# Sigmoid attention and SwiGLU feed-forward: the weights' fp32-to-fp16 conversion moved from VectorE and GpSimd instructions into the weight DMAs

## The chip, the cores and the metric

The kernel runs on one core of one Trainium2 chip. The metric is the device time of one execution in microseconds (us), where lower is better. A profile of one execution, taken by the hardware profiler, accompanies the times. In it PE is TensorE's matmul side, PEld its weight load, DVE is VectorE, ACT is ScalarE, POOL is GpSimd and SP is SyncE, which here issues DMAs only. The names SPq and POOLq stand for DMA-issuing instructions on the queues of those engines.

## The reference

Inputs are `q`, `k`, `v` of shape 8 x 12 x 448 x 64 (batch, heads, sequence, head width) and three weight matrices, all fp32:

```
scores = q @ k.T / sqrt(64) - log(448)
attn   = sigmoid(scores)            # no softmax: every score alone
x      = (attn @ v), heads side by side -> 3584 x 768
g      = x @ w_gate                 # 768 x 1536
val    = x @ w_val                  # 768 x 1536
out    = (g * sigmoid(g) * val) @ w_out      # 1536 x 768 -> 3584 x 768, fp32
```

## The kernel before

**Tiling.** Four heads of one batch make a group, so there are 24 groups `n`, three to a batch. A group has seven tiles `c`. For each tile TensorE computes scores (`qk_tile`, L146), ScalarE takes the sigmoid from PSUM to an fp16 tile `pt` (L157), and after the seventh tile `pv` (L169) multiplies by `v` and VectorE copies the result to the fp16 tiles `xT` (L179). When a batch's three groups are done, the feed-forward runs on it in units: twelve blocks `f` of 128 hidden columns, each with a gate unit and a value unit of six matmuls (L195). The gate unit is followed by a sigmoid on ScalarE (L200) and a product on VectorE (L202), the value unit by a second product on VectorE (L207) that writes `hT`. Output units (L222) follow after each pair of batches. VectorE scales their results to fp32 (L229) and GpSimd's queue stores them (L237).

**Loading q, k and v.** SP issues three DMAs per group (L97), 448 KB each, into six fp32 buffers `st`. VectorE, ScalarE or GpSimd casts each to 16 bit (L115, L117): q and k to bf16 tiles `c`, v to an fp16 tile. q and k are then transposed to tiles `T`: for groups 0 to 5 by TensorE through PSUM (L129) and a VectorE copy (L133), and from group 6 on by a transposing DMA that SP issues (L122).

**Loading weights.** Each of the three matrices comes in six pieces of 768 KB. SP issues the DMA (L81) into one of three fp32 staging buffers `wst`. Later a cast instruction (L87) on VectorE or GpSimd writes the fp16 tiles `wg`, `wv` and `wo` that the matmuls read. These fp16 tiles stay for the whole kernel.

**What sets the order.** The program is written out in one order and every engine works through its own instructions in that order, each waiting for its inputs and for its output buffer to be free. A prologue does the attention of batch 0 (groups 0 to 2). Then a loop over feed-forward units starts, into which two-tile attention steps of later batches are put by a table of nominal unit durations (1.13 and 1.95). Inside the feed-forward of batch 0 the 21 tiles of groups 3 to 5 are spread. The first step with a tile of group 6 comes after the gate unit of block `f` = 9.

SP's order is the list `order`, in which loads of q, k, v and of weights alternate. It is advanced by `loads(...)` calls at fixed points of the prologue and, in the unit loop, after each weight cast and each second tile of a group. A weight load that waits for one of the three staging buffers holds back all that stands behind it in SP's order, and a weight cast that waits for its DMA holds back all that stands behind it on VectorE or GpSimd. In the unit loop, the casts of group `n`+1 are placed at the second tile of group `n`.

Of the kernel before, what the change touches and what calls it, by code (L numbers as in the profile page):

```python
# [17 lines left out]
def kernel(  # L18
# [45 lines left out]
    make_identity(nc, idn)  # L64


    wg16 = [one.tile([128, NP, 256], FP16, tag=f"wg{i}", name=f"wg16_{i}") for i in range(NF // 2)]
    wv16 = [one.tile([128, NP, 256], FP16, tag=f"wv{i}", name=f"wv16_{i}") for i in range(NF // 2)]
    wo16 = [one.tile([128, 2, DM], FP16, tag=f"wo{i}", name=f"wo16_{i}") for i in range(NF // 2)]
    wstage = {}  # L70

    def w_load(kind, i):
        st = wst.tile([128, 1536], FP32, tag="wst", name=f"wst_{kind}{i}")
        if kind == "o":
            src = moe_w_out[i * 256:(i + 1) * 256, :].rearrange("(f p) n -> p f n", p=128)
            dst = st.rearrange("p (f n) -> p f n", f=2)
        else:
            w = moe_w_gate if kind == "g" else moe_w_val
            src = w[:, i * 256:(i + 1) * 256].rearrange("(j p) n -> p j n", p=128)
            dst = st.rearrange("p (j n) -> p j n", j=NP)  # L80
        nc.sync.dma_start(out=dst, in_=src)  # L81
        wstage[(kind, i)] = st

    def w_cast(kind, i, eng):
        dst = {"g": wg16, "v": wv16, "o": wo16}[kind][i]
        st = wstage.pop((kind, i))
        eng.tensor_copy(out=dst.rearrange("p a b -> p (a b)"), in_=st)  # L87


    qkv_st = {}  # L90
# [98 lines left out]

    def ffn1(b, f, gate):  # L190
        ps = psG.tile([128, S], FP32, tag="G", name="ps_g" if gate else "ps_vl")
        w = (wg16 if gate else wv16)[f // 2]
        cs = slice((f % 2) * 128, (f % 2) * 128 + 128)
        for pr in range(NP):
            nc.tensor.matmul(  # L195
                out=ps, lhsT=w[:, pr, cs], rhs=xT[(b, pr)], start=(pr == 0), stop=(pr == NP - 1)
            )
        if gate:
            s16 = tmp.tile([128, S], FP16, tag="s16", name="s16")
            nc.scalar.activation(out=s16, in_=ps, func=SIGM)  # L200
            t1 = tmp.tile([128, S], FP16, tag="t1", name="t1")
            nc.vector.tensor_tensor(out=t1, in0=ps, in1=s16, op=MULT)  # L202
            gcur[0] = t1
        else:
            if b % 2 == 0:
                hT[(b // 2, f)] = htp.tile([128, 2, S], FP16, tag="hT", name=f"hT_{b // 2}_{f}")
            nc.vector.scalar_tensor_tensor(  # L207
                out=hT[(b // 2, f)][:, b % 2, :], in0=ps, scalar=HSC, in1=gcur[0], op0=MULT, op1=MULT
            )
# [3 lines left out]
    def ffn2(b, m, half):  # L213
# [5 lines left out]
        for f in range(NF):  # L219
            h = hT[(b // 2, f)].rearrange("p b s -> p (b s)")  # L220
            lhsT = h[:, m * 128:(m + 1) * 128]
            nc.tensor.matmul(  # L222
                out=o,
                lhsT=lhsT,
                rhs=wo16[f // 2][:, f % 2, half * hw:(half + 1) * hw],
                start=(f == 0),
                stop=(f == NF - 1),
            )
# [49 lines left out]
    NPE = 2 * NJ  # L278


    order = []
    for n in range(NJ):
        order += [(n, 0), (n, 1), (n, 2)]
    order += [("g", 0), ("v", 0), (3, 0), (3, 1), ("g", 1), ("v", 1), (3, 2)]
    order += [("g", 2), ("v", 2), (4, 0), (4, 1), (4, 2), ("g", 3), ("v", 3)]
    order += [(5, 0), (5, 1), (5, 2), ("g", 4), ("v", 4), ("g", 5), ("v", 5)]
    order += [("o", 0), ("o", 1), (6, 0), (6, 1), (6, 2), ("o", 2), ("o", 3), ("o", 4), ("o", 5)]
    order.reverse()

    def loads(n):  # L290
        for _ in range(n):
            if order:
                a, b_ = order.pop()
                if isinstance(a, str):
                    w_load(a, b_)
                else:
                    load(a, b_)


    loads(6)  # L300
# [6 lines left out]
    cast(1, 0, nc.gpsimd)  # L307
    cast(1, 1, nc.vector)
    cast(1, 2, nc.gpsimd)
    loads(3)  # L310
    b0 = [(n, c) for n in range(NJ) for c in range(C)]
    for n, c in b0:
        attn_step([(n, c)], [n - 1] if c == 2 and n > 0 else [])
        if (n, c) == (0, 1):
            trans_pe(1, 0)
            trans_pe(1, 1)
            loads(1)
        if (n, c) == (0, 3):
# [4 lines left out]
        if (n, c) == (1, 1):  # L323
            trans_pe(2, 0)
            trans_pe(2, 1)
        if (n, c) == (1, 3):
            w_cast("g", 0, nc.vector)
            w_cast("v", 0, nc.vector)
            loads(3)
        if (n, c) == (2, 0):  # L330
            cast(3, 0, nc.gpsimd)
            cast(3, 1, nc.gpsimd)
            loads(2)
        if (n, c) == (2, 2):
            w_cast("g", 1, nc.vector)
            w_cast("v", 1, nc.gpsimd)
            cast(3, 2, nc.gpsimd)
            loads(3)
        if (n, c) == (2, 3):
            trans_pe(3, 0)  # L340
            trans_pe(3, 1)
    pv(NJ - 1)


    wcq = [("g", 2), ("v", 2), ("g", 3), ("v", 3), ("g", 4), ("v", 4), ("g", 5), ("v", 5)]
    wcq += [("o", i) for i in range(6)]
    wk = 0
    loaded, casted = 7, 4
    tcur = 0.0
    vi = 0  # L350
    pend = []
    for ui, (dur, u) in enumerate(units):
        while vi < len(visits) and tcur >= vtime[vi]:
            group = visits[vi]
            vi += 1
# [2 lines left out]
            for n, c in group:  # L358
                if c == C - 1:
                    pend.append(n)  # L360
                if c == 1:
                    nn = n + 1
                    loads(3)
# [23 lines left out]
        else:  # L387
            ffn2(*u[1:])
        tcur += dur
        while wcq and ui + 1 >= 1.75 * wk:  # L390
            kind, i = wcq.pop(0)
            w_cast(kind, i, nc.gpsimd if kind == "v" or kind == "o" and i % 2 else nc.vector)
            loads(2)
            wk += 1


# [28 lines left out]
```

## Time and profile before

| | us |
|---|---|
| time, median of 3 (lowest to highest) | 470.07 (469.03 to 471.04) |
| time of the profiled execution | 469.27 |
| its span on the core | 467.5 |
| PE busy | 427.2 (91%) |
| DVE busy | 227.9 (49%) |
| ACT busy | 211.0 (45%) |
| POOL busy | 103.9 (22%) |

The span runs from the first to the last recorded instruction; 1.8 us of the execution's time lies around it. Busy shares are averages over stages that have different limits. The profile also cuts the span into 40 slices of 11.7 us, with the busy tenths of each engine, the clock that TensorE was granted (in tenths of full speed), the busy share of the core's 16 DMA engines and the rate of their transfers. Windows of any length can be asked for in the same form. A chain of waits, followed back from the last instruction, says at each step what released it. A list in order of time gives every instruction's start and duration with, in square brackets, how long its engine sat idle before it and who ended that.

### The profile page before, as it was taken

The page shows a single profiled execution, that of the slowest core. Times are in us where ns is not written, and L with a number is a line of the kernel's source. Part 1 is how long each engine was busy: PE and PEld are TensorE (multiplying, and loading weights), DVE is VectorE, ACT ScalarE, POOL GpSimd, SP SyncE. Part 2 cuts the span into 40 slices and gives each one's busy share as a digit, 9 for nine tenths or more (in the row PEclk, how much of TensorE's full clock was granted, in tenths as well). Part 3 has the DMA queues.
Part 4 walks back from the last instruction along what each step waited for, and adds up shares of the span by engine and source line. Part 5 has one row for each costly group of instructions (what it writes and reads, how often), then busy time and mean ns, then how long its engine had stood idle before and what let it go on. Part 6 is the DMA issues. An engine that isn't in the chain of part 4 may idle for free.

```text
span 467.5 us, 7908 instructions
## 1 busy us (share of the span) xinstructions
PE 427.2 (91%) x3252; PEld 213.9 (46%) x3252; DVE 227.9 (49%) x369; ACT 211.0 (45%) x267; POOL 103.9 (22%) x139
## 2 busy tenths in 40 slices
PE   3779594499999999999999999999999999999993
PEld 2344241244455544444455544444455545555661
DVE  2367373066454355655642454665544356555321
ACT  4776264145643446465534355656543451222000
POOL 2323423620014364100032353200004100000121
PEclk9989888599999999999999999999999999999998
DMA  8986988994006589900027869810014410000232
GB/s 284 349 268 241 355 285 278 306 280 146 1 21 160 165 221 313 281 27 1 1 53 212 237 167 299 237 20 1 1 35 109 101 35 1 1 1 0 68 100 70
DMA packets 66757, 66.97 MB, mean 143 GB/s; under 512 B 35745, under 2 KB 63393, under 8 KB 66721
## 3 DMA queue, kind: packets, MB, share of 16 engines
q1 hardware_dynamic: 64032, 55.45, 40.7%
q0 software_dynamic: 2688, 11.01, 8.7%
q8 instruction: 25, 0.41, 0.3%
q14 instruction: 12, 0.09, 0.1%
HBM read 47.19 MB, written 11.01 MB: 124 GB/s over the span
## 4 chain that ended last, share of the span: by engine, by line
PE 84%; DMA 7%; DVE 3%; ACT 2%; issue 1%; SPq 1%; POOL 1%; POOLq 0%; ACTq 0%; DVEq 0%
PE ps_o L222 24%; PE ps_vl L195 23%; PE ps_g L195 22%; PE ps_sc L146 8%; PE ps_pv L169 6%; ACT pt L157 2%; DMA wst_g<-in_moe_w_gate_dram 2%; DMA wst_o<-in_moe_w_out_dram 2%; DMA st<-in_q_dram 1%; DMA T<-c 1%; PE ps_tr L129 1%; DVE xT L179 1%; SPq L97 1%; DVE hT L207 0%; SPq L122 0%
## 5 line engine op out<-in xcount | busy, mean ns | idle before, releaser
L157 ACT ACTIVATE pt<-ps_sc,sb_t 128x896 f16<-128x896 f32 x168 | 159.7, 1006 | 108.6 <-PE ps_sc L146 108.6
L195 PE MATMUL ps_vl<-xT,wv 128*128 128x448 f16 x576 | 127.1, 357 | 5.1 <-DVE hT L207 5.1
L195 PE MATMUL ps_g<-xT,wg 128*128 128x448 f16 x576 | 126.7, 356 | 1.5 <-DVE xT L179 1.4
L222 PE MATMUL ps_o<-wo,hT 128*128 128x384 f16 x672 | 113.5, 326 | 0.0
L202 DVE TENSOR_TENSOR t<-ps_g,s 128x448 f16<-128x448 f32 x96 | 59.9, 624 | 82.8 <-ACT s L200 81.8
L200 ACT ACTIVATE s<-ps_g 128x448 f16<-128x448 f32 x96 | 52.2, 544 | 106.1 <-PE ps_g L195 106.1
L237 POOL DMA_DIRECT2D out_dram<-osb x56 | 29.2, 525 | 257.3 <-DVE osb L229 257.3
L222 PEld LDWEIGHTS <-hT 128*128 128x128 f16 x672 | 64.0, 98 | 48.6 <-issue 7.9
L195 PEld LDWEIGHTS <-wv 128*128 128x128 f16 x576 | 54.7, 99 | 65.0 <-issue 18.0
L195 PEld LDWEIGHTS <-wg 128*128 128x128 f16 x576 | 54.6, 99 | 58.5 <-issue 12.0
L207 DVE SCALAR_TENSOR_TENSOR hT<-ps_vl,t 128x448 f16<-128x448 f32 x96 | 60.0, 625 | 30.4 <-PE ps_vl L195 22.7
L179 DVE CAST xT<-ps_pv 64x448 f16<-64x448 f32 x96 | 59.7, 622 | 24.4 <-PE ps_pv L169 23.0
L146 PE MATMUL ps_sc<-T,T 64*64 64x448 bf16 x672 | 52.5, 379 | 19.4 <-DMA T<-c 12.7
L229 DVE TENSOR_SCALAR osb<-ps_o 128x384 f32<-128x384 f32 x56 | 31.2, 558 | 74.6 <-PE ps_o L222 74.4
L117 POOL CAST c<-st 128x896 bf16<-128x896 f32 x44 | 40.7, 938 | 38.7 <-DMA st<-in_q_dram 29.7
L169 PE MATMUL ps_pv<-pt,v 64*64 64x448 f16 x672 | 37.3, 357 | 0.3 <-ACT pt L157 0.3
L146 PEld LDWEIGHTS <-T 64*64 64x64 bf16 x672 | 13.8, 107 | 51.1 <-issue 36.6
L117 POOL CAST v<-st 128x896 f16<-128x896 f32 x24 | 22.5, 936 | 35.9 <-PE ps_pv L169 22.4
L169 PEld LDWEIGHTS <-v 64*64 64x64 f16 x672 | 20.4, 109 | 12.9 <-issue 1.3
L129 PE MATMUL ps_tr<-idn,c 128*128 128x128 bf16 x84 | 8.7, 276 | 6.4 <-DVE c L117 4.6
L87 POOL CAST wv<-wst_v 128x1536 f16<-128x1536 f32 x5 | 7.3, 1469 | 18.2 <-DMA wst_v<-in_moe_w_val_dram 18.2
L129 PEld LDWEIGHTS <-c 128*128 128x128 bf16 x84 | 6.9, 125 | 9.4 <-DVE c L117 4.8
(16 smaller groups left out, 27.7 us busy)
## 6 DMA issues: line engine op xcount, KB each, us to landing
st<-in_q_dram SPq DMA_DIRECT2D x24, 448.0 KB, 4.4
st<-in_k_dram SPq DMA_DIRECT2D x24, 448.0 KB, 5.6
st<-in_v_dram SPq DMA_DIRECT2D x24, 448.0 KB, 6.3
out_dram<-osb POOLq DMA_DIRECT2D x56, 192.0 KB, 3.1
wst_g<-in_moe_w_gate_dram SPq DMA_DIRECT2D x6, 768.0 KB, 9.5
wst_v<-in_moe_w_val_dram SPq DMA_DIRECT2D x6, 768.0 KB, 5.1
wst_o<-in_moe_w_out_dram SPq DMA_DIRECT2D x6, 768.0 KB, 4.8
T<-c SPq DMA_TRANSPOSE x36, 5.4
```

Source lines behind the costliest of these rows:

```text
L117: eng.tensor_copy(out=o, in_=i)
L146: nc.tensor.matmul(out=sc[w * 64:(w + 1) * 64, h2, :S], lhsT=kt[r, c, w * 64:(w + 1) * 64], rhs=qt[r, :, w * 64:(w + 1) * 64], start=True, ...
L157: nc.scalar.activation(out=pt, in_=sc[:, :, :S], func=SIGM, bias=sb_t, scale=qkscale)
L169: nc.tensor.matmul(out=P[w][h2 * 64:(h2 + 1) * 64, :], lhsT=vt[r, h2, c * D:(c + 1) * D], rhs=pt[r, h2, :], start=(c == 0), stop=(c == C - 1),
L179: nc.vector.tensor_copy(out=x[w * 64:(w + 1) * 64, :], in_=P[w][h2 * 64:(h2 + 1) * 64, :])
L195: nc.tensor.matmul(out=ps, lhsT=w[:, pr, cs], rhs=xT[(b, pr)], start=(pr == 0), stop=(pr == NP - 1))
L200: nc.scalar.activation(out=s16, in_=ps, func=SIGM)
L202: nc.vector.tensor_tensor(out=t1, in0=ps, in1=s16, op=MULT)
L207: nc.vector.scalar_tensor_tensor(out=hT[(b // 2, f)][:, b % 2, :], in0=ps, scalar=HSC, in1=gcur[0], op0=MULT, op1=MULT)
L222: nc.tensor.matmul(out=o, lhsT=lhsT, rhs=wo16[f // 2][:, f % 2, half * hw:(half + 1) * hw], start=(f == 0), stop=(f == NF - 1),)
L229: nc.vector.tensor_scalar(out=osb[:, half * hw:(half + 1) * hw], in0=o, scalar1=HREC, scalar2=None, op0=MULT)
L237: nc.gpsimd.dma_start(out=dst, in_=osb[i * 64:(i + 1) * 64, :])
```

## The change

The staging buffers `wst`, the DMAs into them and all cast instructions of the weights are removed. GpSimd's queue issues DMAs whose source is the fp32 matrix and whose destination is the fp16 tile. Each matrix now comes in four pieces of 1152 KB (three blocks `f` each) instead of six of 768 KB (two blocks). There are twelve such DMAs. The eight for `w_gate` and `w_val` name 128 x 6 rows of 384 numbers, the four for `w_out` name 128 x 3 rows of 768 numbers.

With this, the schedule of loads is written anew. The number of `st` buffers goes from six to nine. SP's list holds q, k and v loads (and transposes) alone, with three groups loaded ahead. The casts of group `n`+2, no longer of `n`+1, stand at the second tile of group `n`, and with them the transposing DMAs from group 6 on. In the prologue, the first weight DMAs stand on GpSimd behind the casts of q of group 1 and v of group 0, and each later pair behind the casts of the next group. TensorE's transposes of groups 1 and 2 stand two tiles later than before. One cast of k (group 3) goes from GpSimd to VectorE.

```diff
-    stg = ctx.enter_context(tc.tile_pool(name="stg", bufs=6))
-    wst = ctx.enter_context(tc.tile_pool(name="wst", bufs=3))
+    stg = ctx.enter_context(tc.tile_pool(name="stg", bufs=9))
...
+    FW = 3
+    NW = NF // FW
...
     def w_load(kind, i):
-        st = wst.tile([128, 1536], FP32, tag="wst", name=f"wst_{kind}{i}")
...
-        nc.sync.dma_start(out=dst, in_=src)
-        wstage[(kind, i)] = st
-
-    def w_cast(kind, i, eng):
...
-        eng.tensor_copy(out=dst.rearrange("p a b -> p (a b)"), in_=st)
+        cs = slice(i * FW * 128, (i + 1) * FW * 128)
         if kind == "o":
+            nc.gpsimd.dma_start(out=wo16[i], in_=moe_w_out[cs, :].rearrange("(f p) n -> p f n", p=128))
+        else:
+            w, dst = (moe_w_gate, wg16[i]) if kind == "g" else (moe_w_val, wv16[i])
+            nc.gpsimd.dma_start(out=dst, in_=w[:, cs].rearrange("(j p) n -> p j n", p=128))
...
+    load3(0)
+    load3(1)
+    load3(2)
     cast(0, 0, nc.vector)
     cast(0, 1, nc.scalar)
+    cast(1, 0, nc.gpsimd)
     cast(0, 2, nc.gpsimd)
     trans_pe(0, 0)
     trans_pe(0, 1)
...
     cast(1, 1, nc.vector)
+    w_load("g", 0)
+    w_load("v", 0)
+    load3(3)
     cast(1, 2, nc.gpsimd)
...
                 if c == 1:
-                    nn = n + 1
-                    loads(3)
-                    if loaded <= nn + 1 < NQ and not order:
-                        for w in (0, 1, 2):
-                            load(nn + 1, w)
+                    nn = n + 2
+                    if loaded <= nn + 1 < NQ:
+                        load3(nn + 1)
                         loaded = nn + 2
...
+                    for _ in range(2):
+                        if wl:
+                            w_load(*wl.pop(0))
...
-        while wcq and ui + 1 >= 1.75 * wk:
-            kind, i = wcq.pop(0)
-            w_cast(kind, i, nc.gpsimd if kind == "v" or kind == "o" and i % 2 else nc.vector)
-            loads(2)
-            wk += 1
```

Two pieces of the order show what moves. In them `st_6_680` is a staging buffer for group 6 (the last number only names the buffer), `c_0_6` the bf16 tile of q (0) or k (1) of group 6, `v_6` its v, and `T_6` a transposed tile.

On SP, from the loads of group 5 to the transposes of group 6, the rows before are:

```order
L97 DMA st_5_548<-in_v_dram 128x2x448
L81 DMA wst_g_568<-in_moe_w_gate_dram 128x6x256
L81 DMA wst_v_570<-in_moe_w_val_dram 128x6x256
L81 DMA wst_g_582<-in_moe_w_gate_dram 128x6x256
L81 DMA wst_v_584<-in_moe_w_val_dram 128x6x256
L81 DMA wst_o_621<-in_moe_w_out_dram 128x2x768
L81 DMA wst_o_623<-in_moe_w_out_dram 128x2x768
L97 DMA st_6_680<-in_q_dram 128x2x448
L97 DMA st_6_682<-in_k_dram 128x2x448
L97 DMA st_6_710<-in_v_dram 128x2x448
...
L97 DMA st_7_951<-in_v_dram 128x2x448
L122 DMA_TRANSPOSE T_6_957<-c_0_6_953 128x7x128
```

and now:

```order
L88 DMA st_5_454<-in_v_dram 128x2x448
L88 DMA st_6_535<-in_q_dram 128x2x448
L88 DMA st_6_537<-in_k_dram 128x2x448
L88 DMA st_6_539<-in_v_dram 128x2x448
L88 DMA st_7_741<-in_q_dram 128x2x448
L88 DMA st_7_743<-in_k_dram 128x2x448
L88 DMA st_7_745<-in_v_dram 128x2x448
L113 DMA_TRANSPOSE T_6_751<-c_0_6_747 128x7x128
```

All weight loads, ten of them between the loads of group 5 and the transposes of group 6, have left SP's order; the loads of group 7 still stand ahead of the transposes of group 6.

On GpSimd, from its first cast to the casts of group 6, now:

```order
L108 CAST c_0_1_134<-st_1_118 128x2x7x64
L108 CAST v_0_136<-st_0_116 128x896
L78 DMA wg_0_100<-in_moe_w_gate_dram 128x6x384
L78 DMA wv_0_104<-in_moe_w_val_dram 128x6x384
L108 CAST v_1_168<-st_1_122 128x896
L108 CAST c_0_2_218<-st_2_124 128x2x7x64
...
L78 DMA wv_3_107<-in_moe_w_val_dram 128x6x384
L108 CAST c_0_5_541<-st_5_450 128x2x7x64
L108 CAST c_1_5_543<-st_5_452 128x2x7x64
L108 CAST v_5_545<-st_5_454 128x896
L75 DMA wo_0_108<-in_moe_w_out_dram 128x3x768
L75 DMA wo_1_109<-in_moe_w_out_dram 128x3x768
```

Before, the rows of that stretch were casts only, those of q, k and v and five of `wv` (L87). Now eight weight DMAs of `w_gate` and `w_val`, in four pairs, and two of `w_out` stand between the casts, in front of the cast of q of group 6 (`c_0_6`), which comes next.

More of the change, by code (lines that the diff above doesn't have):

```diff
@@ L224, in ffn2 @@
                 lhsT=lhsT,
-                rhs=wo16[f // 2][:, f % 2, half * hw:(half + 1) * hw],
+                rhs=wo16[f // FW][:, f % FW, half * hw:(half + 1) * hw],
                 start=(f == 0),
@@ L278, with load3 @@
     NPE = 2 * NJ
[L281 to L300, printed above, removed]
+    def load3(n):
+        for w in (0, 1, 2):
+            load(n, w)
+    load3(0)
+    load3(1)
+    load3(2)
     cast(0, 0, nc.vector)
     cast(0, 1, nc.scalar)
+    cast(1, 0, nc.gpsimd)
     cast(0, 2, nc.gpsimd)
@@ L313 @@
         attn_step([(n, c)], [n - 1] if c == 2 and n > 0 else [])
-        if (n, c) == (0, 1):
+        if (n, c) == (0, 3):
             trans_pe(1, 0)
             trans_pe(1, 1)
-            loads(1)
-        if (n, c) == (0, 3):
             cast(2, 0, nc.gpsimd)
@@ L321 @@
             cast(2, 2, nc.gpsimd)
-            loads(2)
-        if (n, c) == (1, 1):
+            w_load("g", 1)
+            w_load("v", 1)
+        if (n, c) == (1, 3):
             trans_pe(2, 0)
             trans_pe(2, 1)
[L326 to L330, printed above, removed]
-            cast(3, 0, nc.gpsimd)
[L332 to L336, printed above, removed]
+            load3(4)
+            cast(3, 0, nc.gpsimd)
+            cast(3, 1, nc.vector)
             cast(3, 2, nc.gpsimd)
-            loads(3)
+            w_load("g", 2)
+            w_load("v", 2)
         if (n, c) == (2, 3):
@@ L341 @@
             trans_pe(3, 1)
+            load3(5)
+            cast(4, 0, nc.gpsimd)
+            cast(4, 1, nc.gpsimd)
+            cast(4, 2, nc.gpsimd)
+            w_load("g", 3)
+            w_load("v", 3)
     pv(NJ - 1)
[L345 to L348, printed above, removed]
+    wl = [("o", i) for i in range(NW)]
+    loaded, casted = 6, 5
     tcur = 0.0
@@ L351 @@
     pend = []
-    for ui, (dur, u) in enumerate(units):
+    for dur, u in units:
         while vi < len(visits) and tcur >= vtime[vi]:
```

22 lines of the change are left out of this document (5 added, 17 removed).

## The prediction

> **What bounds the kernel now.** I read the slices of the page first, then windows over the part in which TensorE is not full, then the chain of waits there, and last the list in order of time around the two holes.
>
> ```profile
> PE   3779594499999999999999999999999999999993
> PEclk9989888599999999999999999999999999999998
> DMA  8986988994006589900027869810014410000232
> ```
>
> PE is below 9 only in the first eight slices (94 us) and the last. From there on the clock is at its full value too. The windows give it in numbers (columns: stretch, length, busy us and instructions of PE, PEld, DVE, ACT, POOL, then the granted clock, the DMA share and GB/s):
>
> ```profile
> 97.50:460.00 362.50, 361.92 (x2678) 182.68 (x2676) 182.20 (x300) 159.16 (x207) 68.01 (x98) 1.00 0.40 104
> 34.50:97.50 63.00, 44.22 (x348) 19.84 (x345) 30.43 (x48) 28.86 (x36) 25.20 (x24) 0.84 0.91 297
> 0.00:34.50 34.50, 21.04 (x232) 11.41 (x232) 14.79 (x23) 23.03 (x24) 9.63 (x16) 0.95 0.89 299
> 30.00:40.00 10.00, 7.67 (x83) 3.77 (x81) 7.96 (x13) 6.73 (x9) 3.17 (x4) 0.99 1.04 357
> 10.00:20.00 10.00, 8.01 (x68) 4.28 (x72) 3.75 (x6) 8.34 (x10) 2.81 (x3) 1.00 1.08 370
> ```
>
> From 97.5 us on, TensorE is the bound (361.92 of 362.50 us) and its matmuls do not change. A gain or loss can only be made before that. In 34.5 to 97.5, the feed-forward of batch 0, PE is idle for 18.8 us. There the DMA engines are at a share of 0.91, so they are close to being a second bound: a share near 1 goes with 357 to 370 GB/s. The two holes of PE in that stretch:
>
> ```profile
> 44.89 9.45 DMA wst_g<-in_moe_w_gate_dram
> 67.83 8.19 DMA wst_o<-in_moe_w_out_dram
> 81.51 6.33 DMA T<-c
> ...
> 54.36 0.96 DVE L87 CAST wg<-wst_g 128x1536 f16<-128x1536 f32 x1 [6.09 <-DMA wst_g<-in_moe_w_gate_dram]
> 55.23 0.62 DVE L207 SCALAR_TENSOR_TENSOR hT<-ps_vl,t 128x448 f16<-128x448 f32 x1
> 55.91 2.40 PE L195 MATMUL ps_vl<-xT,wv 128*128 128x448 f16 x6 [5.06 <-DVE hT L207]
> 58.15 4.71 SPq L81 DMA_DIRECT2D wst_o<-in_moe_w_out_dram  x2
> 62.91 0.46 SPq L97 DMA_DIRECT2D st<-in_q_dram  x1
> 64.96 12.98 SPq L81 DMA_DIRECT2D wst_o<-in_moe_w_out_dram  x4
> 79.89 5.46 SPq L122 DMA_TRANSPOSE T<-c  x2
> 87.89 0.59 PE L146 MATMUL ps_sc<-T,T 64*64 64x448 bf16 x4 [12.66 <-DMA T<-c]
> ```
>
> The first hole (5.06 us) is an order problem on VectorE: a weight cast waits 6.09 us for its DMA and holds back the product `hT`, for which PE waits. The second (12.66 us) is one on SP: the transposes of group 6 stand behind the loads of `w_out`, which wait for staging buffers (12.98 us for four), and are issued at 79.89. PE needed them at 87.89 - 12.66 = 75.23. Each hole also costs clock. Just behind them, matmuls run slower than their kind does otherwise:
>
> ```profile
> 58.23 0.96 PE L146 MATMUL ps_sc<-T,T 64*64 64x448 bf16 x8
> 59.13 2.17 PE L195 MATMUL ps_g<-xT,wg 128*128 128x448 f16 x6
> 61.14 1.30 PE L195 MATMUL ps_vl<-xT,wv 128*128 128x448 f16 x6
> 66.03 0.57 PE L146 MATMUL ps_sc<-T,T 64*64 64x448 bf16 x8
> 74.85 0.38 PE L146 MATMUL ps_sc<-T,T 64*64 64x448 bf16 x4
> 88.41 2.42 PE L195 MATMUL ps_vl<-xT,wv 128*128 128x448 f16 x6
> 90.63 1.80 PE L195 MATMUL ps_g<-xT,wg 128*128 128x448 f16 x6
> ```
>
> Behind the first hole that is (2.40 - 1.30) + (0.96 - 0.57) + (2.17 - 1.30) = 2.4 us, behind the second (2.42 - 1.30) + (0.59 - 0.38) + (1.80 - 1.30) = 1.8 us. Both holes with their clock cost 5.06 + 2.4 + 12.66 + 1.8 = 21.9 us. That is the ceiling of the gain.
>
> **Removed: the casts.** By the groups of weight casts below, 18 instructions go: ten on DVE (six of `wg`, one of `wv`, three of `wo`) and eight on POOL.
>
> ```profile
> L87 DVE CAST wg<-wst_g x6: 948/960/1146, 23.8 to 62.5; 128x1536 f16<-128x1536 f32 x6
> L87 POOL CAST wo<-wst_o x3: 1469/1469/1469, 71.6 to 81.9; 128x1536 f16<-128x1536 f32 x3
> ```
>
> That is about 9.6 us of VectorE and 11.8 us of GpSimd. As busy time I count them at nothing, since in 34.5 to 97.5 both engines are under half busy; at most the 0.96 us of a cast or two in PE's way would come back. What counts is that no cast waits in front of `hT` any more: the first hole closes. The weights now have to be there only when PE reads them.
>
> **Moved: SP's order.** Weight loads no longer stand ahead of the loads and transposes of group 6. SP then waits only for `st` buffers, of which there are nine, and for casts, which come one group earlier than before. The second hole closes as far as the bytes can come in time, and this decides the size of the gain.
>
> **The bytes.** PE would reach the transposes of group 6 at 75.23 - 5.06 - 2.4 = 67.8. By then these must have come: q, k and v of groups 0 to 7 (group 7 stands ahead of the transposes on SP), 24 loads of 128 x 2 x 448 fp32 = 0.459 MB, so 11.0 MB; all of `w_gate` (768 x 1536 x 4 bytes) and `w_val` but the last piece's end, 9.4 MB; and the two transposes.
>
> ```profile
> 2.25 6.68 DMA st<-in_q_dram
> q1 hardware_dynamic: 64032, 55.45, 40.7%
> HBM read 47.19 MB, written 11.01 MB: 124 GB/s over the span
> T<-c SPq DMA_TRANSPOSE x36, 5.4
> ```
>
> All transposes took what is left of 40.7% of 467.5 us after reading 47.19 MB at 357 GB/s: 190 - 132 = 58 us, so 1.6 us each with all engines. At 357 GB/s the sum is 2.25 (the second q load's issue, about when the stream is full) + 11.0 MB (30.8 us) + 9.4 MB (26.4 us) + 3.2 = 62.7 us: in time for 67.8. But `wo` pieces 0 and 1 are issued by GpSimd ahead of group 6's casts. If their 2.36 MB (6.6 us) go ahead of the transposes, it is 69.3; if all of `wo` does (13.2 us), 75.9. There is also a fixed delay: group 6's q must land, be cast and be transposed, and a transpose took 5.4 us to land where 1.6 us is its share of engine time. I take 71, so a hole of 3 us in place of 17.7, with 1.8 us of clock behind it. The bounds are no hole at all and 8 us.
>
> One rule speaks against a gain beyond this. The Trainium skill's page "DMA: Bandwidth & Descriptors" (section on issuing engines not being separate DMA queues) says that transfers issued by different engines run on the same 16 DMA engines and interleave, so that a further queue saves issue time only. Here the trace agrees in so far as SP's queue alone reached a share of 1.04 to 1.08. If GpSimd's queue had bandwidth of its own, the transposes would be ready at 2.25 + 30.8 + 3.2 = 36 us and the time would be that of no hole.
>
> **Added: 12 casting DMAs on GpSimd.** The trace has no such DMA. Two costs are unknown.
>
> *Their issue on POOL.* The nearest row is the output store, which names 64 rows of 768 numbers:
>
> ```profile
> L237 POOL DMA_DIRECT2D out_dram<-osb x56: 521/523/662, 138.0 to 461.3; - x56
> 12.66 0.94 POOL L117 CAST c<-st 128x896 bf16<-128x896 f32 x1 [0.37 <-PE ps_sc L146]
> 17.47 1.67 PE L129 MATMUL ps_tr<-idn,c 128*128 128x128 bf16 x14
> 68.39 0.94 POOL L117 CAST c<-st 128x896 bf16<-128x896 f32 x1 [5.93 <-DMA st<-in_q_dram]
> ```
>
> If the cost is fixed it is 0.52 us each. If it goes by rows, 0.523 / 64 x 768 = 6.3 us for a piece of `w_gate` or `w_val` and 3.1 us for one of `w_out`. I take the geometric middle, 1.8 us. The Trainium skill, same page, section on the anatomy of one DMA, calls descriptor generation small and says that many can be emitted before the cost shows; by that it would be the 0.52 us, and the sum would be the same, as follows. Queued behind the first pair on POOL are the cast of v of group 1 and of q of group 2. The latter was done at 13.6, is now done at about 8.98 + 3 x 0.94 + 2 x 1.8 + 0.94 = 16.3, and PE's transposes of group 2 stood at 17.47 and stand later now. So 1.8 us is covered; cover is gone from about 2.5 us on. Later POOL waited longer for loads (5.93 us in the row above) than a pair takes.
>
> *Their rate.* Bytes read are the same 14.2 MB, bytes written are half. If an engine's time goes by the bytes read, weights cost what they cost before; if by the bytes written, half (13.2 us less in the sum above, no hole). Nothing in the trace excludes that the conversion makes it slower; I take twice the engine time as the other end. I take the read bytes, the bound that the loads in the trace show.
>
> **Prologue.** The transposes of group 1 no longer hold up the scores behind them on PE (ACT sat idle 0.64 us for them, below); against this, weights now share the engines from about 11 us on with the loads of groups 2 and 3, which may hold the prologue up by 1 to 3 us. Whatever it loses ahead of group 6 is lost inside the wait for group 6's data, since that comes by bytes. I count nothing.
>
> ```profile
> 12.30 6.40 ACT L157 ACTIVATE pt<-ps_sc,sb_t 128x896 f16<-128x896 f32 x7 [0.64 <-PE ps_sc L146]
> ```
>
> **Sum.** 469.3 (the profiled execution) - 21.9 + 3 + 1.8 = 452.2 us. The median of the runs lies 0.8 above that execution: 453 us.
>
> **Rivals.**
>
> *A. No hole at all.* The DMA engines serve both queues so that group 6 and the weights are in time (62.7 us against 67.8), or writes are what costs. Time 469.3 - 21.9 + 0.8 = 448. For it: the sum without `wo`. Against it: a share of 1 had to be held for 63 us, where it was 0.89 and 0.91.
>
> *B. GpSimd becomes the bound by descriptor generation.* At 6.3 us a piece POOL runs: first pair 9.9 to 22.5, three casts to 25.3, second pair to 37.9, two casts, third pair to 52.4, three casts, fourth pair to 67.8, casts of group 5 to 70.6, two of `wo` to 76.9, casts of q and k of group 6 to 78.8, transposes landed 5.4 to 8 us later, at 84 to 87 where they landed at 87.9. Time 467 to 470, the same as before. For it: the store's 523 ns for only 64 rows. Against it: one size of store cannot tell a fixed cost from one by rows.
>
> *C. Slower: casting DMAs move at half the rate or less.* Place: the DMA engines in the first 100 us. At twice the engine time, the sum is 2.25 + 30.8 + 52.9 + 3.2 = 89.2 us, or 102 with `wo` 0 and 1 ahead, against the 87.9 at which PE went on before: 1 to 14 us slower, middle 478. It decides from a factor f where 36.3 + 26.4 f (+ 6.6 f) = 87.9, so from 1.6 to 2.0; at 3 it is 469 + 28 and more, near 500. For it: the trace has no row that excludes it, and those DMAs write short rows (384 numbers, 768 bytes). Against it: half the bytes written.
>
> *D. A partial slowdown, factor about 1.3:* 36.3 + 34.3 + 8.6 = 79 us, a hole of 11 us, 461.
>
> **How the numbers follow.** The forecast, a hole of up to 8 us, gets 0.44, A 0.14, D 0.14, B 0.09, C 0.19. The time is 453 us. The likeliest case's own range is 448 to 458. The range that holds 8 in 10 runs from 446 (A with a us from the casts or the prologue) to 474, which takes in D and B and the milder part of C and leaves out C beyond a factor of about 1.8. A measurement of this kernel can tell some 0.5% (2.4 us) from no change. Faster: the forecast, A, D (less its worst third) and a little of B: 0.74. Same: most of B, a sliver of C and D: 0.08. Slower: C and a little of B: 0.18.
>
> **What would show it.** Right: no row in which VectorE waits for a weight DMA; the transposes of group 6 issued well ahead of 79.89 and landed near 71; PE's idle time between 34.5 us and its saturated stretch down from 18.8 to a few us; the DMA share there higher than 0.91; that stretch beginning some 17 us earlier, at about 80, and the rest as long as before. The issue of a weight DMA on POOL near 1 to 2 us. Wrong by B: issues near 6 us and POOL busy without gaps until 78. Wrong by C: weight DMAs that take much longer to land than 5 to 10 us with the DMA share at 1 beyond 90 us, PE waiting in `ps_g` or `ps_vl` for DMAs of `wg` or `wv`. My forecast would also be wrong if the rest from 97.5 us on, which I take as unchanged, got holes of its own, since stores and casts of GpSimd stand in another order there.

## The result: 4.5% faster, with both holes gone

| | before | changed |
|---|---|---|
| median of the runs, us (lowest to highest) | 470.56 (469.03 to 471.22) | 449.05 (448.20 to 450.11) |
| ratio to before, 95% interval | | 0.9548 (0.9516 to 0.9581) |
| profiled execution, us | 469.27 | 448.20 |
| its span, us | 467.5 | 446.4 |

One execution among all the runs below, of the kernel with the spread prologue, took 876.97 us, with PE's feed-forward matmuls at 615 to 618 ns where they otherwise take 353; it is left out of that kernel's ratio, and nothing on record says why it happened.

The slices of the page after, in the same form as before:

```profile
PE   2678999999999999999999999999999999999992
PEclk9899999999999999999999999999999999999998
DMA  8999999994284986500278694220033300000242
```

PE reaches 9 in the fifth slice and stays there until the last; before, it did so from the ninth. The windows (stretch, length, busy us and instructions of PE, PEld, DVE, ACT and POOL, clock, DMA share, GB/s):

```profile
0.00:34.50 34.50, 18.92 (x228) 10.68 (x232) 12.59 (x20) 23.12 (x24) 18.24 (x27) 0.95 1.03 294
34.50:97.50 63.00, 61.46 (x514) 28.75 (x505) 38.31 (x62) 39.86 (x52) 17.94 (x21) 1.00 1.19 241
```

In 34.5 to 97.5 us, PE's idle time went from 18.8 to 1.5 us and the clock from 0.84 to 1.00, while the DMA share rose from 0.91 to 1.19. (The share is no plain occupancy, since it can exceed 1: with SP's queue alone, the kernel before reached 1.08.) The prologue did not get shorter: the first gate matmul starts at 34.90 instead of 34.53. A place that both kernels pass, the first gate unit of batch 1, dates the gain:

```profile
99.19 0.35 PE L195 MATMUL ps_g<-xT,wg 128*128 128x448 f16 x1 [0.47 <-DVE xT L179]
```

```profile
77.35 0.35 PE L186 MATMUL ps_g<-xT,wg 128*128 128x448 f16 x1 [0.47 <-DVE xT L170]
```

The first fence is the kernel before, the second the changed one. 21.84 us are gained up to there, of 21.07 in all. The 0.8 us that are lost again behind it were not traced; PE's busy time there is the same (360.69 and 360.70 us), and executions of the changed kernel differ by more (448.20 to 450.11).

What came last, and how close it was, is read from the issues and the landings. The list in order of time of the changed kernel:

```profile
30.82 0.83 POOL L78 DMA_DIRECT2D wv<-in_moe_w_val_dram  x1
43.69 6.66 SPq L113 DMA_TRANSPOSE T<-c  x2
57.59 1.30 PE L186 MATMUL ps_vl<-xT,wv 128*128 128x448 f16 x6
67.64 0.57 PE L137 MATMUL ps_sc<-T,T 64*64 64x448 bf16 x8
68.15 1.31 PE L186 MATMUL ps_vl<-xT,wv 128*128 128x448 f16 x6
```

and of single issues, each with its time to landing: the third and the fourth piece of `w_val`, then the second transpose of group 6.

```profile
L78 POOL DMA_DIRECT2D wv<-in_moe_w_val_dram x1: 826/826/826, 23.8 to 23.8; - x1
DMA to landing us min/median/max: 32.5/32.5/32.5
L78 POOL DMA_DIRECT2D wv<-in_moe_w_val_dram x1: 826/826/826, 30.8 to 30.8; - x1
DMA to landing us min/median/max: 36.3/36.3/36.3
L113 SPq DMA_TRANSPOSE T<-c x1: 5246/5246/5246, 45.1 to 45.1; - x1
DMA to landing us min/median/max: 15.4/15.4/15.4
```

The transposes were there at 45.1 + 15.4 = 60.5, 7 us before the scores at 67.64 that need them. The last weights were not: the third value piece landed at 23.85 + 32.5 = 56.4 for a first use at 57.59, the fourth at 30.82 + 36.3 = 67.1 for 68.15. No hole is left, but with about 1 us to spare at two places.

How much is to spare varies from one execution to the next. In a second profiled execution of the changed kernel (449.04 us, from the last group of runs) the feed-forward begins at 35.77 instead of 34.90. The third value piece landed there at 22.57 + 33.0 = 55.6 for a first use at 58.46, the fourth at 30.70 + 35.0 = 65.7 for 69.02: about 3 us to spare.

### The profile page after: what moved, and what is told of

The parts are those of the page before. It is cut to its first block, busy times and chain, and to the rows that moved or that the text cites. A ratio compares the mean times of both kernels' runs of the same rounds, so it can differ in the third digit from the quotient of the medians.

```text
span 446.4 us, 7870 instructions
## 1 busy us (share of the span) xinstructions
PE 420.9 (94%) x3252; PEld 212.2 (48%) x3252; DVE 220.1 (49%) x360; ACT 210.9 (47%) x267; POOL 100.7 (23%) x142
## 3 DMA queue, kind: packets, MB, share of 16 engines
HBM read 47.19 MB, written 11.01 MB: 130 GB/s over the span
## 4 chain that ended last, share of the span: by engine, by line
PE 92%; ACT 2%; DMA 2%; DVE 1%; issue 1%; POOL 0%; SPq 0%; POOLq 0%; ACTq 0%
PE ps_o L213 25%; PE ps_vl L186 25%; PE ps_g L186 25%; PE ps_sc L137 9%; PE ps_pv L160 7%; ACT pt L148 2%; DMA st<-in_q_dram 2%; PE ps_tr L120 1%; DVE xT L170 1%; SPq L88 0%; POOL c L108 0%; DVE osb L220 0%; POOL out_dram L228 0%; POOLq L391 0%; ACTq L148 0%
## 5 line engine op out<-in xcount | busy, mean ns | idle before, releaser
L186 PE MATMUL ps_g<-xT,wg 128*128 128x448 f16 x576 | 125.4, 353 | 1.5 <-DVE xT L170 1.4
L186 PE MATMUL ps_vl<-xT,wv 128*128 128x448 f16 x576 | 124.9, 353 | 0.0
L186 PEld LDWEIGHTS <-wv 128*128 128x128 f16 x576 | 54.3, 98 | 58.6 <-issue 10.7
L186 PEld LDWEIGHTS <-wg 128*128 128x128 f16 x576 | 54.1, 98 | 57.0 <-issue 9.7
L170 DVE CAST xT<-ps_pv 64x448 f16<-64x448 f32 x96 | 59.7, 622 | 30.8 <-PE ps_pv L160 29.4
L220 DVE TENSOR_SCALAR osb<-ps_o 128x384 f32<-128x384 f32 x56 | 31.2, 558 | 74.6 <-PE ps_o L213 74.4
L137 PE MATMUL ps_sc<-T,T 64*64 64x448 bf16 x672 | 51.1, 370 | 8.8 <-ACT pt L148 7.2
L108 POOL CAST c<-st 128x896 bf16<-128x896 f32 x43 | 39.7, 939 | 54.7 <-DMA st<-in_q_dram 30.3
L137 PEld LDWEIGHTS <-T 64*64 64x64 bf16 x672 | 13.7, 106 | 39.7 <-issue 37.1
L120 PE MATMUL ps_tr<-idn,c 128*128 128x128 bf16 x84 | 7.3, 250 | 6.5 <-DVE c L108 4.7
L120 PEld LDWEIGHTS <-c 128*128 128x128 bf16 x84 | 5.9, 113 | 8.8 <-DVE c L108 4.7
L124 DVE COPY T<-ps_tr 128x896 bf16<-128x896 bf16 x12 | 7.1, 620 | 5.4 <-PE ps_tr L120 5.2
```

The lines of the kernel that those rows point to most:

```text
L108: eng.tensor_copy(out=o, in_=i)
L137: nc.tensor.matmul(out=sc[w * 64:(w + 1) * 64, h2, :S], lhsT=kt[r, c, w * 64:(w + 1) * 64], rhs=qt[r, :, w * 64:(w + 1) * 64], start=True, ...
L170: nc.vector.tensor_copy(out=x[w * 64:(w + 1) * 64, :], in_=P[w][h2 * 64:(h2 + 1) * 64, :])
L186: nc.tensor.matmul(out=ps, lhsT=w[:, pr, cs], rhs=xT[(b, pr)], start=(pr == 0), stop=(pr == NP - 1))
L220: nc.vector.tensor_scalar(out=osb[:, half * hw:(half + 1) * hw], in0=o, scalar1=HREC, scalar2=None, op0=MULT)
```

## Experiments

The medians of the kernel before that ran beside these groups of runs were 470.8, 470.4 and 469.5 us.

### The rate of a casting DMA, measured by itself

A kernel that only moves pieces of 128 x 6 x 384 numbers and stores zeros:

```diff
+    # casting DMAs alone, GpSimd queue
+    for i in range(4):
+        nc.gpsimd.dma_start(out=a16[i], in_=piece(moe_w_gate, i))
+    gate(0, a16, b32)
+    # plain fp32 DMAs alone, GpSimd queue
+    for i in range(4):
+        nc.gpsimd.dma_start(out=b32[i], in_=piece(moe_w_gate, i))
...
+    # plain fp32 DMAs alone, SP queue
+    for i in range(4):
+        nc.sync.dma_start(out=c32[i], in_=piece(moe_w_val, i))
...
+    # casting DMAs (GpSimd queue) beside plain ones (SP queue)
+    for i in range(4):
+        nc.sync.dma_start(out=b32[i], in_=piece(moe_w_val, i))
+        nc.gpsimd.dma_start(out=a16[i], in_=piece(moe_w_gate, i))
```

`gate` reads one number of each of the four pieces, so the next stretch begins when all four have landed.

> This kernel computes nothing of the reference: it stores zeros and only moves weights. Four stretches, one after the other, each of pieces of 128 x 6 x 384 fp32 (1.18 MB read): four converting DMAs from GpSimd's queue alone; four plain fp32 DMAs from GpSimd's queue alone; four plain ones from SP's queue alone; then four converting ones on GpSimd's queue beside four plain ones on SP's. Theory R (engine time goes by the bytes read): the converting pieces land 3.2 to 3.7 us apart, like the plain ones of both queues. Theory W (by the bytes written): 1.7 us apart. Theory C (the conversion costs): 5 us apart or more. In the last stretch, equal shares would put both kinds 6.5 to 7 us apart; if SP's queue goes first, its pieces keep 3.5 us and the converting ones wait behind them.

VectorE reads one number of each piece as soon as it has landed, so its idle times give the spacing. In the list in order of time, the second and third landing of the first three stretches (casting alone, fp32 from GpSimd alone, fp32 from SP alone) and the first three landings of the casting pieces beside SP's:

```profile
10.37 0.15 DVE L44 CAST gate<-a 128x1 f32<-128x1 f16 x1 [2.69 <-DMA a<-in_moe_w_gate_dram]
13.27 0.15 DVE L44 CAST gate<-a 128x1 f32<-128x1 f16 x1 [2.75 <-DMA a<-in_moe_w_gate_dram]
...
26.36 0.15 DVE L44 COPY gate<-b 128x1 f32<-128x1 f32 x1 [3.00 <-DMA b<-in_moe_w_gate_dram]
29.53 0.15 DVE L44 COPY gate<-b 128x1 f32<-128x1 f32 x1 [3.01 <-DMA b<-in_moe_w_gate_dram]
...
42.10 0.15 DVE L44 COPY gate<-c 128x1 f32<-128x1 f32 x1 [3.01 <-DMA c<-in_moe_w_val_dram]
45.26 0.15 DVE L44 COPY gate<-c 128x1 f32<-128x1 f32 x1 [3.01 <-DMA c<-in_moe_w_val_dram]
...
61.09 0.15 DVE L44 CAST gate<-a 128x1 f32<-128x1 f16 x1 [11.97 <-DMA a<-in_moe_w_gate_dram]
67.46 0.15 DVE L44 CAST gate<-a 128x1 f32<-128x1 f16 x1 [6.22 <-DMA a<-in_moe_w_gate_dram]
73.86 0.15 DVE L44 CAST gate<-a 128x1 f32<-128x1 f16 x1 [6.25 <-DMA a<-in_moe_w_gate_dram]
```

Alone, a casting piece takes 2.90 us (1.18 MB read, so 407 GB/s of reading), an fp32 piece 3.17 us from either queue (372 GB/s). The conversion costs no DMA time; halving the bytes written gains 8%, not half. So theory R holds nearly, and rival C has no ground. With both queues full, the casting pieces come 6.4 us apart, and SP's fp32 pieces, by their issues and landings (55.0, 61.2, 67.6 and 74.0 us), 6.2 to 6.4 us apart as well: equal shares. The changed kernel's weight landings, 4 to 8 us apart, are of that kind. The page's GB/s row shows 202 to 203 for the casting stretch, half of what is read, so it counts the bytes written. That is one reason why the window from 34.5 us shows fewer GB/s at a higher share after the change.

### GpSimd's queue in the old schedule, with and without the conversion

First the conversion, which moves the queue as well: the kernel before, its `w_load` issuing casting DMAs on GpSimd's queue in the same order and the casts left out.

```diff
-        nc.sync.dma_start(out=dst, in_=src)
-        wstage[(kind, i)] = st
+        nc.gpsimd.dma_start(out={"g": wg16, "v": wv16, "o": wo16}[kind][i], in_=src)
...
     def w_cast(kind, i, eng):
+        return
```

> The kernel before with the conversion alone moved: the weights' DMAs (pieces of 768 KB as before) are converting ones on GpSimd's queue, at the places of the program where SP issued them; six st buffers and the casts one group ahead stay. Theory S (leaving SP's queue and having no cast to wait for is what counts): both holes close or shrink, with the transposes of group 6 landing at 72 to 79 us for a need at 73, so 449 to 457 us. Rival (the rewritten schedule of loads and casts carries the gain): 462 us or more, with the second hole still over 8 us.

457.14 us, ratio 0.9711 (0.968 to 0.9742), just past the slow end of theory S's range (457) and far from the rival's. Group 6's second transpose landed at 58.6 + 17.0 = 75.6, as theory S had it. What is left against the changed kernel, in PE's list of time: a hole for group 6's transposes, and a feed-forward that begins 3.05 us later than at 34.90.

```profile
37.95 1.40 PE L188 MATMUL ps_g<-xT,wg 128*128 128x448 f16 x5
75.65 0.59 PE L139 MATMUL ps_sc<-T,T 64*64 64x448 bf16 x4 [4.57 <-DMA T<-c]
```

Then the queue without the conversion: plain fp32 DMAs into the three staging buffers from GpSimd's queue, each behind the cast that frees its buffer, with the casts kept.

```diff
     def w_load(kind, i):
+        if len(wstage) == 3:
+            wheld.append((kind, i))
+            return
...
-        nc.sync.dma_start(out=dst, in_=src)
+        nc.gpsimd.dma_start(out=dst, in_=src)
...
         eng.tensor_copy(out=dst.rearrange("p a b -> p (a b)"), in_=st)
+        if wheld:
+            w_load(*wheld.pop(0))
```

> The kernel before with the queue alone moved: weights come as plain fp32 DMAs into the three staging buffers and are cast by instructions as before, but GpSimd's queue issues the DMAs, each behind the cast that frees its buffer; SP has q, k and v alone. Theory S (no staging and no cast to wait for is needed): the second hole closes in part, but casts on VectorE and GpSimd go on waiting for DMAs and hold back what stands behind them, so 455 to 468 us, the first hole there still. Rival (any queue other than SP's does it): 452 us or less.

456.25 us, ratio 0.9698 (0.9663 to 0.9734), as theory S had it. The first hole is still there, with the same chain, but smaller, and a cast of `w_out` makes another one by holding back `xT`:

```profile
53.37 0.96 DVE L90 CAST wg<-wst_g 128x1536 f16<-128x1536 f32 x1 [2.95 <-DMA wst_g<-in_moe_w_gate_dram]
54.92 1.29 PE L200 MATMUL ps_vl<-xT,wv 128*128 128x448 f16 x6 [1.53 <-DVE hT L212]
66.12 0.96 DVE L90 CAST wo<-wst_o 128x1536 f16<-128x1536 f32 x1 [2.50 <-DMA wst_o<-in_moe_w_out_dram]
68.93 1.29 PE L200 MATMUL ps_g<-xT,wg 128*128 128x448 f16 x6 [1.32 <-DVE xT L184]
74.39 0.38 PE L151 MATMUL ps_sc<-T,T 64*64 64x448 bf16 x4 [0.97 <-DMA T<-c]
```

So taking the weights out of SP's queue is about two thirds of the gain (13.7 us with the conversion and 14.6 without, of 21.5), and in the old schedule the conversion adds nothing to that.

### The new schedule without the conversion

The changed kernel's schedule, with six `st` buffers, fp32 DMAs of 768 KB from GpSimd's queue into three staging buffers, and casts at the pace of the kernel before.

```diff
-    stg = ctx.enter_context(tc.tile_pool(name="stg", bufs=9))
+    stg = ctx.enter_context(tc.tile_pool(name="stg", bufs=6))
+    wst = ctx.enter_context(tc.tile_pool(name="wst", bufs=3))
...
-    FW = 3
+    FW = 2
...
+    def w_cast(kind, i, eng):
+        dst = {"g": wg16, "v": wv16, "o": wo16}[kind][i]
+        st = wstage.pop((kind, i))
+        eng.tensor_copy(out=dst.rearrange("p a b -> p (a b)"), in_=st)
+        w_load()
...
+        while wcq and ui + 1 >= 1.75 * wk:
+            kind, i = wcq.pop(0)
+            w_cast(kind, i, nc.gpsimd if kind == "v" or kind == "o" and i % 2 else nc.vector)
+            wk += 1
```

> The changed kernel with the conversion undone: its schedule of q, k and v (casts two groups ahead, SP's queue free of weights; six st buffers, which cost nothing when undone alone) is kept, and the weights come as plain fp32 DMAs of 768 KB from GpSimd's queue into three staging buffers, cast by VectorE and GpSimd, each DMA behind the cast that frees its buffer. Theory S (casts that wait for DMAs hold back VectorE and GpSimd, and three buffers hold back the DMAs): waits of VectorE or PE for weights of 1 to 6 us come back, 451 to 457 us. Rival (queue and schedule are all of it, the conversion in the DMA adds nothing): 450 us or less.

462.49 us, ratio 0.9842 (0.982 to 0.9864): worse than either theory had it, and worse than the old schedule with the same staging (456.25). PE has three holes of about 2 us and more. GpSimd now casts two groups in a row, and VectorE's weight cast beside it is stretched (2.21 us). Then a weight cast waits for its DMA and holds back `hT`, as in the kernel before (1.93 us). Later, one waits for `w_out` and holds back `xT` (4.16 us):

```profile
38.47 1.81 POOL L125 CAST c<-st 128x896 bf16<-128x896 f32 x2
39.11 5.48 DVE L94 CAST wg<-wst_g 128x1536 f16<-128x1536 f32 x1
40.22 0.93 POOL L125 CAST v<-st 128x896 f16<-128x896 f32 x1
41.09 1.80 POOL L125 CAST c<-st 128x896 bf16<-128x896 f32 x2
42.85 0.92 POOL L125 CAST v<-st 128x896 f16<-128x896 f32 x1
45.17 0.55 PE L137 MATMUL ps_tr<-idn,c 128*128 128x128 bf16 x7 [2.21 <-DVE hT L215]
...
55.34 0.96 DVE L94 CAST wg<-wst_g 128x1536 f16<-128x1536 f32 x1 [3.35 <-DMA wst_g<-in_moe_w_gate_dram]
56.88 2.36 PE L203 MATMUL ps_vl<-xT,wv 128*128 128x448 f16 x6 [1.93 <-DVE hT L215]
...
72.46 0.96 DVE L94 CAST wo<-wst_o 128x1536 f16<-128x1536 f32 x1 [4.92 <-DMA wst_o<-in_moe_w_out_dram]
75.27 2.40 PE L203 MATMUL ps_g<-xT,wg 128*128 128x448 f16 x6 [4.16 <-DVE xT L187]
```

The casting DMAs and the new schedule thus depend on each other. With staging, the new schedule costs 6 us; with casting DMAs it gains 8 (457.14 to 449.05). Within the new schedule, the conversion is worth 14 us (462.49 against 448.74 for the changed kernel with six `st` buffers, below). This holds for the places that the staged casts were given here; other places for them were not tried.

### Which part of the schedule

Three runs undo the number of buffers, the lead of the casts, and both.

```diff
-    stg = ctx.enter_context(tc.tile_pool(name="stg", bufs=9))
+    stg = ctx.enter_context(tc.tile_pool(name="stg", bufs=6))
```

> The changed kernel with six st buffers, as before, and nothing else undone. Theory M (of the rewritten schedule it is the casts two groups ahead that close the second hole; the buffers only let SP's queue run further ahead, which takes engine time from the weights): group 6 is still in time for its need near 73 us and the weights land a little earlier, 447 to 451 us. Rival (nine buffers are what brings group 6 in time): its transposes land after 73 us, PE waits 4 us or more for them, 453 to 458 us.

448.74 us, ratio 0.9539 (0.9515 to 0.9563): nothing lost.

```diff
-                    nn = n + 2
-                    if loaded <= nn + 1 < NQ:
-                        load3(nn + 1)
-                        loaded = nn + 2
+                    nn = n + 1
+                    if loaded <= nn + 2 < NQ:
+                        load3(nn + 2)
+                        loaded = nn + 3
```

> The changed kernel with the casts and transposes of the unit loop one group ahead, as before, and nine buffers with loads three groups ahead kept. Theory M: the cast of q of group 6 moves from 42.7 us to about 60, the transposes land 12 to 20 us after that, at 72 to 80 for a need near 73: a hole of 0 to 7 us, 450 to 457 us. Rival (the lead does nothing, the loads were what was late): 448 to 450 us.

449.39 us, ratio 0.9561 (0.9537 to 0.9586): nothing lost either, against theory M. Its reason was wrong: I had taken the place of a cast in the program for its time. GpSimd runs ahead of PE, and cast q of group 6 at 44.60 us here, not at 60. Its second transpose landed at 51.0 + 15.6 = 66.6 instead of 60.5. So the lead does bring group 6 earlier, by 6 us, but the 7 us of room that group 6 has take that up.

> The changed kernel with both undone: six buffers and casts one group ahead. What then differs from the kernel before with only the conversion moved (457.1 us) is the size of the pieces (1152 instead of 768 KB) and the order of the prologue. Theory M: the lead is the larger part, so about as in the run with the lead alone undone, 450 to 457 us. Rival (the prologue and the size of the pieces carry the rest of the gain): 451 us or less.

455.12 us, ratio 0.9671 (0.9643 to 0.9699). Each alone costs nothing, both together 6 us. SP's list shows why:

```profile
46.68 0.37 SPq L88 DMA_DIRECT2D st<-in_q_dram  x1
47.55 0.37 SPq L88 DMA_DIRECT2D st<-in_k_dram  x1
48.42 0.37 SPq L88 DMA_DIRECT2D st<-in_v_dram  x1
48.84 10.45 SPq L113 DMA_TRANSPOSE T<-c  x2
...
72.65 0.59 PE L137 MATMUL ps_sc<-T,T 64*64 64x448 bf16 x4 [3.88 <-DMA T<-c]
```

With the lead undone, group 8's loads stand ahead of group 6's transposes on SP; with six buffers these loads wait for group 6's casts. The first transpose then goes at 48.84 instead of 43.69, and the second, issued at 54.1 behind the bytes of group 8, lands at 54.1 + 18.5 = 72.6, when PE goes on. This is the second hole of the kernel before, in small: on SP, a transpose stands behind a load that waits for a buffer. What is left between this run and the old schedule with casting DMAs (457.14) is 2 us, for the order of the prologue and the larger pieces together; the two were not told apart.

### How much room the weights have

```diff
+            w_load("o", 0)
+            w_load("o", 1)
             w_load("g", 3)
             w_load("v", 3)
...
-    wl = [("o", i) for i in range(NW)]
+    wl = [("o", i) for i in range(2, NW)]
```

> The changed kernel with the first two pieces of w_out issued ahead of the last pieces of w_gate and w_val. Theory M (the weights were the last to come and had about 1 us to spare: the last piece of w_val landed at 67.1 us and was read at 68.2): two pieces more at 6.5 us each make the last pair land at 74 and 80 us, PE waits 7 us for the gate piece and about 5 us more for the value piece and loses clock: 460 to 464 us. Rival (the weights have room and group 6 is what limits): 448 to 451 us.

459.45 us (455.79 to 460.91), ratio 0.977 (0.9731 to 0.9808). PE waits where theory M said, for 6.5 instead of 12 us in the profiled execution, the fastest of the four:

```profile
67.21 1.31 PE L186 MATMUL ps_g<-xT,wg 128*128 128x448 f16 x6 [1.09 <-DMA wg<-in_moe_w_gate_dram]
74.43 2.42 PE L186 MATMUL ps_vl<-xT,wv 128*128 128x448 f16 x6 [5.42 <-DMA wv<-in_moe_w_val_dram]
```

The last value piece landed at 31.3 + 43.1 = 74.4, 7 us later than without the edit. I had charged the two pieces the pace of a shared queue (6.5 us each); the delay is that of about 3.7 us each, nearer to the 2.9 us of a piece that has the engines alone.

### A shorter prologue

The `pv` matmuls of groups 0 and 1 are spread over three tiles, and a group's two transposes stand two tiles apart.

```diff
...
-        attn_step([(n, c)], [n - 1] if c == 2 and n > 0 else [])
+        sc = qk_tile(n, c)
+        if n > 0 and c == 1:
+            pv(n - 1, 0, 3)
+        if n > 0 and c == 2:
+            pv(n - 1, 3, 5)
+        if n > 0 and c == 3:
+            pv(n - 1, 5, C)
+        sig_tile(n, c, sc)
+        if (n, c) == (0, 4):
+            trans_pe(1, 1)
+        if n > 0 and c == 5:
+            trans_pe(n + 1, 1)
...
```

> The changed kernel with a prologue in which ScalarE starves less: the attn-times-v matmuls of groups 0 and 1 are spread over three tiles instead of standing in one block of 28, and the two transposes of a group are put two tiles apart. ACT sat idle about 3 us for these blocks, so the feed-forward could begin 1 to 3 us earlier. Theory D (the weights' landing, 56.4 us for the third value piece and 67.1 for the fourth, with 1 us of room, is now the bound of the feed-forward of batch 0): PE waits for wv by what the prologue gains beyond 1 us, so 448 to 449.5 us. Rival (it still has room): 446 to 447.5 us.

448.84 us (median of five, 447.00 to 450.18), ratio 0.9541 (0.9515 to 0.9567), not to be told from the changed kernel's 0.9548. That is in theory D's range and outside the rival's. The list in order of time comes from another execution of the same kernel:

> The same kernel as the one with the spread prologue, for its list in order of time. Theory D: the feed-forward begins 1 to 3 us before 34.9 and PE then waits up to 2 us for the third or fourth value piece. Rival: no wait for wv, and the feed-forward begins less than 1 us earlier.

```profile
33.07 1.40 PE L195 MATMUL ps_g<-xT,wg 128*128 128x448 f16 x5
66.54 0.87 PEld L195 LDWEIGHTS <-wv 128*128 128x128 f16 x6 [0.57 <-DMA wv<-in_moe_w_val_dram]
```

The feed-forward begins 1.8 us earlier, and PE's weight load then waits 0.57 us for the fourth value piece: theory D's wait, at the short end of what it allowed. This execution took 446.59 us, and beside the changed kernel's second profiled execution (35.77) its feed-forward begins 2.7 us earlier. Then the same with six `st` buffers, beside the unaltered changed kernel:

```diff
-    stg = ctx.enter_context(tc.tile_pool(name="stg", bufs=9))
+    stg = ctx.enter_context(tc.tile_pool(name="stg", bufs=6))
```

> The spread prologue together with six st buffers. With six buffers the last value piece landed at 65.5 instead of 67.1 us. Theory D (weights bound what the prologue can gain): 1 to 2 us under the changed kernel beside it, about 447 us. Rival (the spread prologue gains nothing on its own): the same within 0.3%.

> The changed kernel itself, unaltered, beside the three others on one chip: 448 to 450 us.

447.36 us, ratio 0.9524 (0.9506 to 0.9543), beside 449.31 us, ratio 0.9566 (0.9549 to 0.9583). It has the lowest median of the kernels here, 0.4% under the changed one, as theory D had it. Neither edit alone (ratios 0.9541 and 0.9539) can be told from the changed kernel or from both together, so which of them carries the gain is open. The landing at 65.5 us, which the expectation credits to six buffers, is not shown to come from them: with nine it was 65.7 in the second profiled execution.

## Why the prediction was right, and where its size was off

**The bound and the two holes: right.** All of the gain lies ahead of the saturated stretch, and both holes and their slow clock went. The ceiling was 21.9 us, the profiled executions differ by 21.1.

**The term that was off: the remaining hole.** The forecast had 3 us of hole and 1.8 us of clock behind it, since I took 71 us for the arrival of group 6's transposes. They were there at 60.5. That makes 4.8 us, of which 453 against 449.05 shows 4. The outcome is that of rival A (448), to which I gave a chance of 0.14. My argument against A, that a DMA share of 1 would have to be held for 63 us, did not hold: the share was 1.03 and then 1.19. The step that failed is the sum of bytes as one line: it put all of the weights ahead of the transposes and then added pieces of `w_out` as well. The two queues have separate lines and an equal share when both are full (6.4 us a piece in the rate run). SP's line was the one that was early and the weights' line the one that ended last, at 67.1. When the transposes were there, seven of the eight pieces of `w_gate` and `w_val` had come (the seventh landed at 30.0 + 30.6 = 60.6), and none of `w_out`. With these seven alone, 8.3 MB, the same sum at 357 GB/s is 2.25 + 30.8 + 23.1 + 3.2 = 59.4 us (an estimate), near the measured 60.5. So the rate fits, and what was wrong is which bytes stood ahead.

**The byte sum itself** gave 62.7 us for everything that was needed by 67.8, and the last of it landed at 67.1. The "no hole" branch was nearer than I judged, but the room was 1 us in this execution and 3 us in the second, and 7 us more of weights ahead brought a hole back.

**Issue on GpSimd:** taken at 1.8 us, measured 0.82 to 0.97 for 768 rows and 0.75 for 384, beside 0.53 for 64. Between 64 and 768 rows that is 0.4 ns a row. Rival B's price of a piece (6.3 us) was nearly eight times too high. The Trainium skill's page "DMA: Bandwidth & Descriptors", in its section on the anatomy of one DMA, calls descriptor generation small and says that many can be emitted before the cost shows; these rows agree.

**Two queues:** the Trainium skill's page "DMA: Bandwidth & Descriptors", in its section on issuing engines not being separate DMA queues, says that DMAs of different engines run on the same 16 DMA engines and that a further queue saves issue time only. On the shared engines the traces agree: with both queues full, a piece took 6.4 us where it took 2.9 alone. That only issue time is saved does not hold here: SP's queue was held back by weight loads that waited for buffers, and moving these to GpSimd's queue gave 14.6 us with staging and casts as before.

**Rate:** taken at the read bytes (357 GB/s); measured alone, 407 GB/s of reading. Rivals C and D needed a factor of 1.3 and more; it is 0.92 of an fp32 piece.

**Prologue:** taken at nothing, measured 0.4 us later, and 1.2 in the second profiled execution. In the old schedule with casting DMAs, the feed-forward began 3.4 us later than before, so that cost is real, and the new schedule avoids most of it.

**Removed casts:** counted at nothing as busy time, which no run here contradicts; as waits they were the first hole, and they came back where the weights were staged, in the old schedule (1.53 us) and in the new one (1.93 us).

## What to carry to other kernels

Look at what each DMA queue holds in order before counting its bytes: about two thirds of this gain came from taking weight loads that wait for buffers out of the queue in which transposes stood behind them, and the same fault came back in small (6 us) when two settings that were harmless one by one were undone together. A conversion that a DMA can do while it moves the data costs no DMA time here and removes both the staging buffers and the in-order waits of the casting engines; it is worth trying with the schedule that these waits had forced, since neither paid in full without the other. When the holes are closed, ask what lands last and with how much room, and ask it of more than one execution: here 1 us in one and 3 us in another, and a shorter prologue then waited 0.57 us for that landing.

## What the runs showed of the hardware that I had not expected

A VectorE cast from fp32 in SBUF to 16 bit, 0.96 us by itself, took 5.48 us in the new schedule with staging, while GpSimd ran six casts back to back; it ended 0.8 us after the last of them (42.85 + 0.92 = 43.77 against 44.59). Two shorter overlaps end the same way. In this run a VectorE cast of 1.72 us ends at 48.02, 0.8 us after the GpSimd cast that had begun before it (45.71 + 1.48 = 47.19); in the kernel before, one of 1.15 us ends at 43.58 after a GpSimd cast that ended at 42.77. The Trainium skill's page "SBUF — State Buffer", section on who interferes with whom, says that VectorE in its two-port modes and GpSimd share one pair of ports and that the one that comes second is blocked for the whole instruction. The traces agree on the block, but here it lasted for a series of GpSimd instructions, not for one; no row names the mode in which VectorE ran. It is one more reason why the staged weights did badly in the new schedule, and not the whole one: of the 8.3 us of PE's three holes there, 2.21 stand behind the stretched cast.
